# Expert rows turned by transposing transfers instead of TensorE, and another order of the last two batches' routing, in an attention and mixture-of-experts kernel

## The chip, the cores and the metric

The kernel runs on one core of a Trainium2 chip. The metric is the device time of one execution in microseconds (us). Engines are named as in the profile: PE (TensorE), PEld (its weight loads), DVE (VectorE), ACT (ScalarE), POOL (GpSimd) and SP (SyncE, which here only issues transfers).

## The reference

Chunked attention with memory keys, and then a mixture of experts with two experts for each token:

```
for each chunk c of 32 positions:              # 4 batches, 8 heads, 768 positions, head size 64
    keys   = 8 memory keys + positions c-16 .. c+32+8
    out[c] = softmax(q[c] @ keys.T / 8) @ values
x = out as 3072 rows of 512
noisy  = x @ w_gate + log1p(exp(x @ w_noise)) * noise          # 8 experts
top2   = the two largest of each row; gates = softmax over the two
y[row] = sum over its two experts e of gate * (relu(x[row] @ w1[e]) @ w2[e])   # w1 512x1024, w2 1024x512
```

## The kernel before, in words

**Attention** works in 16 pairs of heads (NPAIR = 16, four for each of the 4 batches), in a software pipeline written out by hand: the loop over `i` issues, for each engine in turn, steps of pairs `i+2`, `i+1`, `i`, `i-1` and `i-2`. For the change these matter, all of a pair `n`: `PT_pe` (L323) transposes the probabilities P on PE, `PT_dve` (L330) copies them out of PSUM, `PV_pe` (L335) multiplies them with the values, `mult_dve` (L349) divides by the sums and writes the rows `xrow`, `xT_pe` (L363) transposes these rows on PE and lets ACT copy them to `xt`, for the logits. The PSUM pool for transposes has three buffers, that for PV's result one.

**Routing** of a batch `b` starts with `logits_pe` (L374) and runs as small steps (`s1` to `s8`, L392 to L517): noise scale (`ns`, on ACT), noisy logits `nl`, comparison of all pairs of experts (`df`, `bt`), the two best (`two`), a one-hot `oh` over the 28 pairs of experts, ranks by matmuls with a triangular matrix (`s3`, `s5`), a table of places (`s5b` builds `Rn`, `s6` multiplies, `s7` adds to the running table `tab`), and the gates (`s4`), which are written to HBM with the rows. `s8` adds the batch's counts to `seen`. The steps of batches 0 to 2 hang in a list `pending` and are dealt out between the steps of the attention (`early_steps`, `late_steps`); those of the last batch run in one go after the last pair (L649 to L661).

**Buckets.** A token's two experts are one of 28 pairs, and each pair is a bucket of up to 128 rows. A bucket is fetched once: `gather` (L693, POOL) fetches its rows from HBM by index, `turn` (L701) transposes the 128 rows of 512 on PE in four pieces, DVE copies them to `xTb`, and ACT copies the gates to `meta`. The first 122 places of a bucket are its own; overflow goes to spill places that are handled apart.

**Experts** run in order 0 to 7. Each has seven buckets, in a big half (4) and a small half (3). `first` (L758) multiplies w1 with a half's rows (8 blocks of 128 hidden units, 4 matmuls each, into four PSUM buffers `ps_h`), and ACT and DVE take turns at the relu. `second` (L777) multiplies one bucket with w2; a bucket that comes for the first time is copied to one of 20 accumulators by ACT, one that comes for the second time is added by DVE and scattered to the output by POOL, with a small transfer `spart` by SP. Expert `e` meets 7, 6, 5, 4, 3, 2, 1 and 0 buckets that no expert before had (`plan[e]`). In the kernel before, expert `e` gathers `plan[e+1]` after its first products (L902 to L904), then loads w1 of expert `e+2`, turns one new bucket after each second product (L911), and loads w2 of expert `e+2` at its end. All gathers, scatters and weight loads are issued by POOL, in this order.

Of the kernel before, what the change touches and what calls it, by code (L numbers as in the profile page):

```python
# [24 lines left out]
def kernel(  # L25
# [73 lines left out]
    def body():  # L99
# [49 lines left out]
        def zero_v(x, j, eng=None):  # L149
            (eng or nc.vector).memset(vbufs[x][:, 6 * j:6 * j + 6], 0.0)  # L150
# [178 lines left out]

        def PT_dve(n):  # L330
            PT = ap_.tile([128, 2 * UB, 128], BF16, name="PT")
            nc.vector.tensor_copy(PT, st[n]["p_p"])  # L332
            st[n]["PT"] = PT

        def PV_pe(n):  # L335
# [27 lines left out]
        def xT_pe(n):  # L363
            b, r = divmod(n, HP)
            y, half = divmod(r, 2)
            p_x = psT.tile([128, UB, 2, 128], BF16, name="p_x", tag="tr")
            for u in range(UB):
                for s in range(2):
                    nc.tensor.transpose(out=p_x[:, u, s, :], in_=xrows[b][:, UB * half + u, 128 * y + 64 * s:128 * y + 64 * s + 64].bitcast(BF16), identity=identb)  # L369
            xt = ap_.tile([128, UB, 2, 128], BF16, name="xt", bufs=5)  # L370
            nc.scalar.copy(xt, p_x)  # L371
            st[n]["xt"] = xt

        def logits_pe(b):  # L374
# [12 lines left out]
        def route(b):  # L387
# [4 lines left out]
            def s1():  # L392
                ns = T("ns", [128, BT, E])
                ps_l = logits[b]
                nc.scalar.activation(out=ns, in_=ps_l[:, :, E:], func=Act.Exp)
                nc.scalar.activation(out=ns, in_=ns, func=Act.Ln, bias=1.0)
                R["ns"] = ns
                R["lg"] = T("lg", [128, BT, E])
                nc.scalar.copy(R["lg"], ps_l[:, :, :E])

# [34 lines left out]
            def s2b():  # L435
                over = T("over", [128, BT, E])
                nc.vector.tensor_reduce(out=over, in_=R["bt"], axis=AX, op=Alu.add)
                two = T("two", [128, BT, 2, E], BF16)
                nc.vector.tensor_scalar(out=two, in0=over.rearrange("p t (o e) -> p t o e", o=1).to_broadcast([128, BT, 2, E]),
                                        scalar1=2.0, scalar2=None, op0=Alu.is_lt)  # L440
                oh = T("oh", [128, BT, E // 2, E], BF16)
                tw = two.rearrange("p t o e -> p t (o e)")
                pitch = tw.ap[1][0]
                win = bass.AP(tw.tensor, tw.offset + 1, [list(tw.ap[0]), [pitch, BT], [1, E // 2], [1, E]])
                side.tensor_tensor(out=oh, in0=two[:, :, 0:1, :].to_broadcast([128, BT, E // 2, E]), in1=win, op=Alu.mult)
                R["two"] = two[:, :, 0, :]
                R["oh"] = oh.rearrange("p t d e -> p t (d e)")

# [120 lines left out]
        def late_steps():  # L569
            if pending:  # L570
                for fn in pending.pop(0)[1]:
                    fn()
# [18 lines left out]
        for i in range(NPAIR):  # L591
            if i >= 1:
                PT_pe(i - 1)
            max_dve(i)
            for n in ahead(i):
                qkT_pe(n)
            fresh = i >= 3 and (i - 3) % HP == HP - 1
            if fresh:
                begin_route((i - 3) // HP)
            early_steps()  # L600
            if i >= 1:
                PT_dve(i - 1)
            sub_dve(i)
            if i == 0:
                zero_v(1, 1)
                load_v(1)
                new_group(3)
                load_qk(3)
            if i == 1:
                zero_k(3)  # L610
            for n in ahead(i):
                kT_act(n)
            if i >= 1:
                PV_pe(i - 1)
            if i + 1 < NPAIR:
                scores_pe(i + 1)
            if i < NPAIR - 1:
                late_steps()
            if i in (2, 3, 4):
                zero_v(2, i - 2)  # L620
            if i >= 1:
                mult_dve(i - 1)
                if i - 1 == NPAIR - 2:
                    write_rows(B, B - 1, 0, UB, 0, XC)
            if i >= 2:
                xT_pe(i - 2)
            if i == 2:
                load_v(2)
                memory_values(2, NG)
            for n in ahead(i):  # L630
                g = n // GP + 3
                if n % GP == 1 and g < NG:
                    new_group(g)
                    load_qk(g)
            if i == 3:
                zero_v(2, 3, nc.gpsimd)
                ramps()
                load_router()
            if i == 4:
                load_v(3)  # L640
            if i == 5:
                constants()
            if i >= 4 and i % GP == 0 and i // GP + 2 < NG:
                load_v(i // GP + 2)
            if i == GP * (NG - 3) + 1:
                load_w1(0)
                load_w2(0)
                load_w1(1)
        n = NPAIR - 1  # L649
        PT_pe(n)  # L650
        PT_dve(n)
        xT_pe(n - 1)
        late_steps()
        PV_pe(n)
        mult_dve(n)
        write_rows(B + 1, B - 1, UB, BT, 0, XC)
        early_steps()
        xT_pe(n)
        late_steps()
        begin_route(B - 1)  # L660
        late_steps()  # L661


        tab = tabs[(B - 1) % 2]
        gidx = rp.tile([128, NB], I32, name="gidx")
# [35 lines left out]
        def turn(p, other=False):  # L701
            xl = got[p]
            p_t = psY.tile([128, KP, CAP], BF16, name="p_t2", tag="ps_y") if other else psX.tile([128, KP, CAP], BF16, name="p_t")
            for kp in range(KP):
                nc.tensor.transpose(out=p_t[:, kp, :], in_=xl[:, kp * 64:(kp + 1) * 64].bitcast(BF16), identity=identb)  # L705
            nc.vector.tensor_copy(xTv[:, :, p, :], p_t)  # L706
            nc.scalar.copy(meta[:, p, :], xl[:, XC:].bitcast(F32))

        def gather_spill(s_gi):
            xl = ld.tile([128, ROW], I32, name="xl")  # L710
# [166 lines left out]
        for e in range(E):  # L877
            big, small = halves(e)
            if e == E - 1:
                end = nc.values_load(n_spill_i[0:1, 0:1], min_val=SPILL, max_val=N)  # L880
                past = xg.tile([128, NP], F32, name="past")
                nc.vector.tensor_scalar(out=past, in0=srank, scalar1=-float(SPILL), scalar2=None, op0=Alu.add)
            ht = hp_.tile([128, FB, (E - 1) * CAP], BF16, name="ht")
            if e == 0:
                parts = [big[:2], big[2:], small]
                off = 0
                for x, ps in enumerate(parts):
                    for j, p in enumerate(ps):
                        turn(p, j % 2 == 1)
                    if x == 2:  # L890
                        turn_spill()
                        find_tails()
                    first(W1[e], ht, off, ps, nc.scalar if x == 0 else None, CAP if x == 2 else OWN, big if x == 2 else ())
                    off += len(ps)
                    if x == 0:
                        s_gi, s_si = find_spill()
                        gather_spill(s_gi)
                        load_w2(1)
            else:
                first(W1[e], ht, 0, big)  # L900
                first(W1[e], ht, len(big), small)
            nxt = list(plan[e + 1]) if e + 1 < E else []  # L902
            for p in nxt:
                gather(p)  # L904
            if e + 2 < E:
                load_w1(e + 2)
            order = big + small

            for j, p in enumerate(order):
                second(e, p, ht, j, W2[e])  # L910
                if nxt:  # L911
                    turn(nxt.pop(0))
                if e == E - 1 and j == 1:
                    for x in range(1, E // 2 - 1):
                        nc.vector.tensor_tensor(out=spart[:, 0, :], in0=spart[:, 0, :], in1=spart[:, x, :], op=Alu.add)
            if e == E - 1:
                assert color(order[-1]) >= NCOL
                nc.vector.tensor_tensor(out=spart[:, 0, :], in0=spart[:, 0, :], in1=spart[:, E // 2 - 1, :], op=Alu.add)
                nc.gpsimd.indirect_dma_start(
                    out=out_part[NB], out_offset=bass.IndirectOffsetOnAxis(ap=s_si[:, 0:1], axis=0),  # L920
                    in_=spart[:, 0, :], in_offset=None, bounds_check=N - 1, oob_is_err=False)
            while nxt:
                turn(nxt.pop(0))
            if e + 2 < E:
                load_w2(e + 2)
        return end, past, ovc, ramp_i, onesb, identb, psX, psY, first, ld, hp_, xg, accs, load_w1, load_w2, W1, W2, relu, psH
# [87 lines left out]
```

## Time and profile before

| | |
|---|---|
| median of 3 runs | 337.96 us (335.78 to 338.23) |
| profiled execution | 335.33 us |
| its span in the profile | 333.7 us |
| granted TensorE clock, mean | 0.957 |
| attention and routing, up to the first gather | 0 to 114.2 us |
| expert 0 starts its first products | 119.8 us |
| experts 1, 2, 3 start | 152.6, 177.9, 203.1 us |
| bytes moved by DMA | 42.99 MB, mean 129 GB/s |

How to read it: the span is the time from the first to the last instruction in the trace of one execution. A group of instructions is named by its line, engine, operation and tiles (written<-read). "Idle before" is the time that the engine stood still just before, and the arrow names what ended that. The chain of waits follows the work back from the last instruction, always to what released it; "issue" in it is time in which nothing in the profile was waited for. In windows of the trace, times are us from the span's start.

### The profile page before, as it was taken

The page shows a single profiled execution, that of the slowest core. Times are in us where ns is not written, and L with a number is a line of the kernel's source. Part 1 is how long each engine was busy: PE and PEld are TensorE (multiplying, and loading weights), DVE is VectorE, ACT ScalarE, POOL GpSimd, SP SyncE. Part 2 cuts the span into 40 slices and gives each one's busy share as a digit, 9 for nine tenths or more (in the row PEclk, how much of TensorE's full clock was granted, in tenths as well). Part 3 has the DMA queues.
Part 4 walks back from the last instruction along what each step waited for, and adds up shares of the span by engine and source line. Part 5 has one row for each costly group of instructions (what it writes and reads, how often), then busy time and mean ns, then how long its engine had stood idle before and what let it go on. Part 6 is the DMA issues. An engine that isn't in the chain of part 4 may idle for free.

```text
span 333.7 us, 7301 instructions
## 1 busy us (share of the span) xinstructions
PE 288.1 (86%) x3019; PEld 173.5 (52%) x3019; DVE 169.9 (51%) x343; ACT 133.4 (40%) x235; POOL 138.6 (42%) x181
## 2 busy tenths in 40 slices
PE   1697887977776377999999999999999999999990
PEld 0575675755654256554754754544544544544540
DVE  7789859849958775222322323424342433434451
ACT  7877788757433033533333332332303303202200
POOL 7877868538023472781008007007152042042152
PEclk9999999979989559999999999999999999999997
DMA  7999999999997136699407905914959624521031
GB/s 99 179 163 176 184 163 163 210 143 101 214 225 216 23 88 93 128 156 238 87 0 125 221 4 110 223 28 105 207 147 166 117 111 70 86 109 60 1 140 71
DMA packets 58763, 42.99 MB, mean 129 GB/s; under 512 B 32449, under 2 KB 52033, under 8 KB 58728
## 3 DMA queue, kind: packets, MB, share of 16 engines
q0 software_dynamic: 49808, 38.71, 77.0%
q1 hardware_dynamic: 8632, 3.74, 5.6%
q8 instruction: 24, 0.39, 0.5%
q10 hardware_dynamic: 288, 0.07, 0.1%
q14 instruction: 11, 0.09, 0.1%
HBM read 61.23 MB, written 10.66 MB: 215 GB/s over the span
## 4 chain that ended last, share of the span: by engine, by line
PE 43%; issue 24%; DVE 13%; ACT 8%; POOL 7%; DMA 3%; POOLq 0%; DVEq 0%; ACTq 0%
PE ps_h L769 16%; PE ps_y L780 14%; POOL out_dram L788 4%; ACT kd L276 3%; PE ps_o L345 3%; DMA out_dram<-acc,sidx 2%; PE ps_o L341 2%; DVE mx L313 2%; DVE xrow L358 2%; DVE sd L318 2%; DVE vg L150 2%; PE p_t L705 2%; ACT xt L371 1%; ACT P L320 1%; PE p_t L265 1%
## 5 line engine op out<-in xcount | busy, mean ns | idle before, releaser
L769 PE MATMUL ps_h<-xTb,w1t 128*128 128x512 bf16 (+5 forms) x640 | 101.4, 320 | 1.5 <-DVE xTb L706 1.5
L780 PE MATMUL ps_y<-w2t,ht 128*128 128x512 bf16 x448 | 101.4, 379 | 0.0
L769 PEld LDWEIGHTS <-w1t 128*128 128x128 bf16 x640 | 58.6, 99 | 43.9 <-DVE xTb L706 1.1
L788 POOL DMA_INDIRECT out_dram<-acc,sidx x28 | 28.1, 1004 | 126.4 <-DVE acc L787 124.1
L756 DVE TENSOR_SCALAR ht<-ps_h 128x512 bf16<-128x512 f32 (+3 forms) x68 | 38.1, 560 | 68.1 <-PE ps_h L769 63.1
L780 PEld LDWEIGHTS <-ht 128*128 128x128 bf16 x448 | 42.9, 98 | 46.7
L754 ACT ACTIVATE ht<-ps_h 128x384 bf16<-128x384 f32 (+2 forms) x76 | 38.9, 511 | 70.4 <-PE ps_h L769 66.3
L784 ACT ACTIVATE acc<-ps_y,meta 128x512 f32<-128x512 f32 x28 | 19.2, 687 | 62.6 <-PE ps_y L780 45.4
L787 DVE SCALAR_TENSOR_TENSOR acc<-ps_y,meta,acc 128x512 f32<-128x512 f32 x28 | 21.0, 750 | 34.5 <-PE ps_y L780 34.5
L696 POOL DMA_INDIRECT xl<-x_rows,gidx x28 | 30.0, 1071 | 16.8 <-PE ps_h L769 6.6
L134 POOL DMA_DIRECT2D vg<-in_v_dram x34 | 25.5, 756 | 11.4 <-DMA kg<-in_k_dram 3.7
L706 DVE COPY xTb<-p_t 128x512 bf16<-128x512 bf16 x28 | 11.6, 422 | 28.6 <-PE p_t L705 28.4
L276 ACT COPY kd<-p_t 64x768 bf16<-64x768 bf16 x32 | 25.2, 786 | 1.0 <-PE p_t L265 0.8
L265 PE MATMUL p_t<-identb,qg 128*64 128x128 bf16 x192 | 10.3, 245 | 12.0 <-DMA qg<-in_q_dram 6.6
L371 ACT COPY xt<-p_x 128x768 bf16<-128x768 bf16 x16 | 12.8, 798 | 12.0 <-PE p_x L369 11.9
L341 PE MATMUL ps_o<-memv,PT 128*128 128x260 bf16 x96 | 15.0, 296 | 2.2 <-DVE PT L332 2.0
L320 ACT ACTIVATE P<-sd 128x768 bf16<-128x768 f32 x16 | 13.5, 845 | 8.1 <-DVE sd L318 8.1
L268 ACT COPY qT<-p_t 128x768 bf16<-128x768 bf16 x16 | 12.8, 800 | 8.9 <-PE p_t L265 8.8
L358 DVE TENSOR_TENSOR xrow<-ps_o,rec 128x768 bf16<-128x768 f32 x16 | 15.3, 958 | 0.6
L313 DVE TENSOR_REDUCE mx<-ps_s 128x12 f32<-128x768 f32 x16 | 15.1, 942 | 0.5 <-PE ps_s L300 0.5
L318 DVE TENSOR_TENSOR sd<-ps_s,mx 128x768 f32<-128x768 f32 x16 | 15.2, 949 | 0.0
L345 PE MATMUL ps_o<-vg,PT 128*32 128x256 bf16 x384 | 14.9, 293 | 0.0
(150 smaller groups left out, 287.5 us busy)
## 6 DMA issues: line engine op xcount, KB each, us to landing
w1t<-in_moe_w_dram POOLq DMA_DIRECT2D x8, 1024.0 KB, 11.4
w2t<-in_moe_w_dram POOLq DMA_DIRECT2D x8, 1024.0 KB, 10.1
vg<-in_v_dram POOLq DMA_DIRECT2D x30, 168.0 KB, 10.2
qg<-in_q_dram POOLq DMA_DIRECT2D x7, 384.0 KB, 9.9
kg<-in_k_dram POOLq DMA_DIRECT2D x7, 384.0 KB, 11.3
x_rows<-xrow SPq DMA_DIRECT2D x3, 792.0 KB
x_rows<-xrow SPq DMA_DIRECT2D x2, 384.0 KB
xl<-x_rows,gidx POOLq DMA_INDIRECT x28, 6.5
```

Of the source, the lines that this page charges most:

```text
L134: nc.gpsimd.dma_start(out=vg[p0 + j:p0 + j + nj, c:c + n, hd, :, :].rearrange("p c e d -> p c (e d)"), in_=bass.AP(v.tensor, v.offset + (g ...
L276: nc.scalar.copy(st[n]["kT"][hs, hh, :].rearrange("d (p j) -> d p j", j=SJ), st[n]["p_k"][hs].rearrange("d j p -> d p j"))
L313: nc.vector.tensor_reduce(out=mx, in_=st[n]["ps"], axis=AX, op=Alu.max)
L318: nc.vector.tensor_tensor(out=sd, in0=st[n]["ps"], in1=bc4(st[n]["mx"], CTX), op=Alu.subtract)
L345: nc.tensor.matmul(out=po[32 * r:32 * r + 32, u, :MD], lhsT=PT[:, 2 * u + e, 32 * r:32 * r + 32], rhs=vg[:, CB * half + x, :, e, :], start ...
L358: nc.vector.tensor_tensor(out=xr.rearrange("p u (h d) -> p u h d", d=D), in0=po[:, :, :MD].rearrange("p u (h d) -> p u h d", d=D), in1=rec ...
L696: nc.gpsimd.indirect_dma_start(out=xl, out_offset=None, in_=xd, in_offset=bass.IndirectOffsetOnAxis(ap=idx[:, p:p + 1], axis=0), bounds_ch ...
L754: nc.scalar.activation(out=dst, in_=src, func=Act.Relu)
L756: nc.vector.tensor_scalar(out=dst, in0=src, scalar1=0.0, scalar2=None, op0=Alu.max)
L769: nc.tensor.matmul(out=ps_h[:, o:o + w], lhsT=w1t[:, kp, f * 128:(f + 1) * 128], rhs=rhs(kp), start=(kp == 0 and i == 0), stop=(kp == KP - ...
L780: nc.tensor.matmul(out=ps_y, lhsT=ht[:, f, j * CAP:(j + 1) * CAP], rhs=w2t[:, f, :], start=(f == 0), stop=(f == FB - 1))
L788: nc.gpsimd.indirect_dma_start(out=out_part[p], out_offset=bass.IndirectOffsetOnAxis(ap=sidx[:, p:p + 1], axis=0), in_=a, in_offset=None, ...
```

## The change

Two edits that have nothing to do with each other.

1. Buckets of experts 2 to 6 are no longer turned on PE. `turn_far` gathers a bucket and lets SP issue four transposing transfers from the gathered rows straight into `xTb`; it is called two experts ahead, where `turn` was called one expert ahead (`plan[1]` stays with `turn`). In expert 0 the first two such buckets come before the second products. ACT copies the gates of these buckets at the expert's end. w1 of expert `e+2` is now loaded ahead of the gathers.
2. In the seam between attention and experts, the order of batch 2's and batch 3's routing is written out: batch 2's `s1m`, `s2a`, `s2g` ahead of `mult_dve` of pair 14, the others between the last pair's steps, `s6` after the last logits and `s7` inside batch 3's steps. The transpose of rows of pair 13 goes behind P's of pair 15. P of pair 15 is copied by ACT, one third of the last `xt` by DVE. The last batch's logits are read from PSUM without a copy, and its one-hot is made by POOL instead of DVE.

```
         def PT_dve(n):
-            nc.vector.tensor_copy(PT, st[n]["p_p"])
+            (nc.scalar.copy if n == NPAIR - 1 else nc.vector.tensor_copy)(PT, st[n]["p_p"])
...
         def xT_pe(n):
-            nc.scalar.copy(xt, p_x)
+            own = UB - 1 if n == NPAIR - 1 else UB
+            nc.scalar.copy(xt[:, :own], p_x[:, :own])
+            if own < UB:
+                nc.vector.tensor_copy(xt[:, own:], p_x[:, own:])
...
             def s1():
+                if b == B - 1:
+                    R["lg"] = ps_l[:, :, :E]
+                    return
...
             def s2b():
-                side.tensor_tensor(out=oh, ...)
+                nc.gpsimd.tensor_tensor(out=oh, ...)
...
+            if i == NPAIR - 1:
+                s1m, s2a, s2g, s2b, s4b, s3, s4, s5, s5b, s6, s7, s8 = [f for pair in pending for part in pair for f in part]
+                pending.clear()
+                s1m()
+                s2a()
+                s2g()
             if i >= 1:
                 mult_dve(i - 1)
...
-            if i >= 2:
+            if 2 <= i < NPAIR - 1:
                 xT_pe(i - 2)
...
         PT_pe(n)
         PT_dve(n)
-        xT_pe(n - 1)
-        late_steps()
+        xT_pe(n - 2)
+        s2b()
+        s4b()
+        s4()
         PV_pe(n)
         mult_dve(n)
         write_rows(B + 1, B - 1, UB, BT, 0, XC)
-        early_steps()
+        xT_pe(n - 1)
+        s3()
+        s8()
+        s5()
         xT_pe(n)
-        late_steps()
-        begin_route(B - 1)
-        late_steps()
+        s5b()
+        logits_pe(B - 1)
+        begin, (_, (s1n, s1m, s2d, s2a, s2g, s2b, s4b, s3, s4, s5, s5b, *last)) = route(B - 1)
+        begin()
+        s6()
+        for f in (s1n, s1m, s2d, s2g, s2a, s2b, s4b, s7, s3, s4, s5, s5b, *last):
+            f()
...
+        def turn_far(p):
+            gather(p)
+            for kp in range(KP):
+                nc.sync.dma_start_transpose(out=xTv[:, kp, p, :], in_=got[p][:, kp * 64:(kp + 1) * 64].bitcast(BF16))
...
-            nxt = list(plan[e + 1]) if e + 1 < E else []
+            nxt = list(plan[1]) if e == 0 else []
             for p in nxt:
                 gather(p)
+            far = list(plan[e + 2]) if e + 2 < E else []
             if e + 2 < E:
                 load_w1(e + 2)
+            if e == 0:
+                for p in far[:2]:
+                    turn_far(p)
...
             for j, p in enumerate(order):
                 second(e, p, ht, j, W2[e])
                 if nxt:
                     turn(nxt.pop(0))
+                late = j + 2 if e == 0 else j
+                if late < len(far):
+                    turn_far(far[late])
...
-            while nxt:
-                turn(nxt.pop(0))
+            for p in far:
+                nc.scalar.copy(meta[:, p, :], got[p][:, XC:].bitcast(F32))
             if e + 2 < E:
                 load_w2(e + 2)
```

More of the change, by code (lines that the diff above doesn't have):

```diff
@@ L444, in s2b @@
                 win = bass.AP(tw.tensor, tw.offset + 1, [list(tw.ap[0]), [pitch, BT], [1, E // 2], [1, E]])
-                side.tensor_tensor(out=oh, in0=two[:, :, 0:1, :].to_broadcast([128, BT, E // 2, E]), in1=win, op=Alu.mult)
+                nc.gpsimd.tensor_tensor(out=oh, in0=two[:, :, 0:1, :].to_broadcast([128, BT, E // 2, E]), in1=win, op=Alu.mult)
                 R["two"] = two[:, :, 0, :]
```

## The prediction

> **What bounds the kernel now.** I read the page first (engine shares, the 40 slices), then the busy time by stage, then the chain of waits inside the expert stage, then the timeline of the seam between attention and experts, and last the transfers by window. The page, parts 1 and 2:
>
> ```profile
> PE 288.1 (86%) x3019; PEld 173.5 (52%) x3019; DVE 169.9 (51%) x343; ACT 133.4 (40%) x235; POOL 138.6 (42%) x181
> ...
> PE   1697887977776377999999999999999999999990
> ...
> PEclk9999999979989559999999999999999999999997
> DMA  7999999999997136699407905914959624521031
> ```
>
> A slice is 8.34 us. From slice 16 on (133 us) PE is full; slices 12 to 15 (100 to 133 us) are the seam. By stage (busy us and instructions of PE, PEld, DVE, ACT, POOL, then clock, DMA share, GB/s):
>
> ```profile
> 107.00:114.24 7.24, 2.02 (x26) 1.58 (x27) 6.32 (x28) 0.24 (x1) 1.15 (x2) 0.51 0.25 70
> ...
> 152.40:177.90 25.50, 25.50 (x174) 14.73 (x173) 7.78 (x14) 8.91 (x19) 2.19 (x3) 1.00 0.45 101
> 177.90:203.10 25.20, 25.20 (x170) 14.43 (x168) 8.21 (x14) 8.13 (x17) 6.45 (x7) 1.00 0.61 116
> ```
>
> Two regimes. In the seam (first row) DVE works 6.32 of 7.24 us in a serial chain and PE idles. In the experts PE is busy for all 25.5 and 25.2 us of experts 1 and 2: there, only PE time taken away counts, or a new wait of PE. The chain of waits there:
>
> ```profile
> 152.55 12.19 PE ps_h L769 x96
> 164.74 1.73 PE ps_y L780 x8
> 166.47 0.22 PE p_t L705 x4
> 166.69 1.73 PE ps_y L780 x8
> ...
> 174.49 3.45 PE ps_y L780 x16
> 177.94 12.19 PE ps_h L769 x96
> ...
> 197.93 5.18 PE ps_y L780 x24
> 203.11 3.02 PE ps_h L769 x14
> ```
>
> An expert is 12.19 us of first products and seven second products of 1.73 us; each block of rows turned on PE (four p_t transposes) adds 0.22 us, with no gap.
>
> **The change, part 1: blocks of experts 2 to 6.** New blocks per expert are 7, 6, 5, 4, 3, 2, 1, 0; so 5+4+3+2+1 = 15 turns leave PE. Each is 0.22 us on the chain: 15 x 0.22 = 3.3 us gained. The 15 copies of xTb leave DVE, which waits for PE there and gives nothing. ACT's copies of the gates (meta) stay, moved to an expert's end. The ends of the kernel (last scatters) follow PE and move with it.
>
> What it adds: 15 x 4 = 60 transposing transfers on SP's queue, of which this trace has none. Call T the time from one to the next. What T must be follows from the start and the deadlines, so I look at loads and gathers. Timeline of POOL, then DMA issues of five windows (141 to 143.5 us, 143.5 to 150.3, 182.5 to 184, 134 to 142, last column landing time), then SP's timeline, the size of its meta transfers, its L548, and last the end of expert 3 in the whole chain:
>
> ```profile
> 141.94 0.83 POOL L538 DMA_DIRECT2D w1t<-in_moe_w_dram  x1
> ...
> 149.42 1.01 POOL L696 DMA_INDIRECT xl<-x_rows,gidx  x1 [0.30 <-issue]
> ```
> ```profile
> w2t<-in_moe_w_dram POOLq DMA_DIRECT2D x1, 1024.0 KB, 13.1
> ```
> ```profile
> xl<-x_rows,gidx POOLq DMA_INDIRECT x5, 10.2
> ```
> ```profile
> w1t<-in_moe_w_dram POOLq DMA_DIRECT2D x1, 1024.0 KB, 10.0
> ```
> ```profile
> xl<-x_rows,gidx POOLq DMA_INDIRECT x6, 2.9
> ```
> ```profile
> 128.79 4.70 SPq L730 DMA_DIRECT2D meta<-xl  x6
> ```
> ```profile
> meta<-xl SPq DMA_DIRECT2D x6, 0.2 KB
> ```
> ```profile
> L548 SPq DMA_DIRECT2D x_rows<-xrow x6: 359/362/371, 58.8 to 111.2; - x6
> ```
> ```profile
> 221.07 6.91 PE ps_y L780 x32
> ```
>
> Start. In the kernel before, expert 2's gathers go out at 144 to 150 us behind both weight loads and land 10.2 us later. Now only w1 of expert 2 lies ahead (issued 141.94, landing some 10.0 later, 152); w2 goes behind the gathers. With the seam's 0.8 us (part 2) the first gather lands near 151 to 152, the last near 155.5 (estimate: five of them in the 4 us or so that they took behind w2, which landed at 142.74 + 13.1 = 155.9). So transposing starts at about 152, and from there the queue always has work: expert 1's first four steps scatter nothing, so POOL runs on into expert 3's gathers.
>
> Deadlines. Expert 2's big half needs four blocks, 16 transfers, at 177.94 - 0.8 - 5 x 0.22 = 176.0: T up to (176.0 - 152)/16 = 1.50 us. Its fifth block is due 7 us later: 31/20 = 1.55. Expert 3 has all four new blocks in its big half, 36 transfers in all, due at 203.11 - 0.8 - 9 x 0.22 = 200.3: T up to 48.3/36 = **1.34 us**, the tightest. Expert 4's three are in its small half, 48 transfers by about 221.07 + 6.91 - 0.8 - 12 x 0.22 + 5 = 229: 1.6. So up to T = 1.34 all is hidden; beyond it PE stalls 36 us for each us of T, and at T = 1.34 + 3.5/36 = 1.44 the gain is gone.
>
> Bounds of T from rows: below, SP's own 0.36 us per issue of a big transfer (L548); above, 2.9 us, a gather that lands with nothing ahead of it, as if each transfer waited for the one before. Nearest by queue, size and issue back to back are the six meta transfers, 4.70/6 = 0.78 us. I take T below 1.34, near that row and not near 2.9, and cost it at nothing on PE; the cover is expert 1 and half of expert 2, and with it gone the price is that of rival 2. A transposing transfer of 32 KB has more to do than a 0.2 KB one, so both ends stay in the range.
>
> The Trainium skill ("VectorE: DVE Perf Modes", section "The three transpose paths") gives 390 ns for a 128x128 bf16 transpose on TensorE and 1309 ns through DMA. The trace disagrees on the first: four of them cost 0.22 us on the chain, so 60 would be worth 23.4 us by the page and 3.3 by the row, and the row decides. On the second no row speaks; with it 152 + 36 x 1.309 = 199.1 would be 1.2 us ahead of expert 3, an estimate that leaves the sum as it is.
>
> SP's queue carries also the 24 spart transfers; those of expert 1 stand behind expert 3's transposes. Their readers are the reuse of an accumulator two experts on and the sum in expert 7, so nobody is late.
>
> A wait that is added: ACT's gate copies at the end of expert 0 stand ahead of expert 1's relus and wait for the last gather, near 155.5. PE starts expert 1 at 152.55 - 0.8 and fills four ps_h in 4 x 12.19/16 = 3.0 to 3.5 us, by 155.2; the first relu (ACT's) then ends near 156.3. The stall is 0 to 1.1 us: I take 0.6. For later experts the gathers go out ten and more us before the copies: nothing.
>
> **Part 2: the seam.** Rows of the timeline:
>
> ```profile
> 97.31 0.84 ACT L320 ACTIVATE P<-sd 128x768 bf16<-128x768 f32 x1 [2.22 <-DVE sd L318]
> ...
> 98.91 0.82 PE L369 MATMUL p_x<-identb,xrow 128*128 128x128 bf16 x6
> ...
> 99.52 0.85 PE L327 MATMUL p_p<-identb,P 128*128 128x128 bf16 x6
> ```
> ```profile
> 99.77 0.80 ACT L371 COPY xt<-p_x 128x768 bf16<-128x768 bf16 x1 [1.61 <-PE p_x L369]
> ...
> 100.41 0.56 DVE L332 COPY PT<-p_p 128x768 bf16<-128x768 bf16 x1
> ...
> 102.69 0.51 POOL L445 TENSOR_TENSOR oh<-two 128x192 bf16<-128x192 bf16 x1 [7.63 <-DVE two L439]
> ...
> 102.98 0.96 DVE L358 TENSOR_TENSOR xrow<-ps_o,rec 128x768 bf16<-128x768 f32 x1
> ...
> 104.54 0.80 ACT L371 COPY xt<-p_x 128x768 bf16<-128x768 bf16 x1 [2.72 <-PE p_x L369]
> ...
> 105.53 1.07 DVE L480 TENSOR_SCALAR Rn<-ramp,rank_all 128x128 bf16<-128x128 bf16 x6
> ...
> 106.14 0.24 ACT L396 ACTIVATE ns<-ns 128x48 f32<-128x48 f32 x1
> ...
> 106.90 0.19 DVE L503 TENSOR_TENSOR tab<-ps_t,tab 128x28 f32<-128x28 f32 x1 [0.31 <-PE ps_t L495]
> 107.01 0.20 DVE L407 TENSOR_TENSOR nl<-ns,nz_all 128x48 f32<-128x48 f32 x1
> ...
> 109.93 0.27 DVE L445 TENSOR_TENSOR oh<-two 128x192 bf16<-128x192 bf16 x1
> ...
> 114.24 1.19 POOL L696 DMA_INDIRECT xl<-x_rows,gidx  x1 [2.82 <-DVE ov L807]
> ```
>
> - P copy by ACT, p_x of pair 13 behind it: P is ready at 98.15, so p_p starts near 98.95 instead of 99.52. ACT copies in 0.80 (as its xt row) where DVE took 0.56 but came only at 100.41: PT at 100.6 instead of 100.97, 0.35 us gained, carried on to the last xrow (103.94 to 103.6).
> - Batch 2's s1m and s2a go into DVE's idle time before 99; s2b and s4 fill the time up to the last xrow: nothing.
> - The last xt is shared, 512 columns on ACT (0.6 by the 0.80 row's share) and 256 on DVE: 0.2 us, so logits come 0.55 us early. The logits are no longer copied; ns, which ended at 106.38, ends near 105.85.
> - s7 leaves its place before the last batch's nl, which waited for Rn (to 106.60), s6 and tab (106.90). Now nl follows ns and Rn: 105.9 instead of 107.01, 1.1 us gained. s7 lies under the one-hot, where DVE idles.
> - The one-hot by POOL: 0.51 instead of 0.27, on the path to rank: 0.3 us lost with the hand-over. oht and ohp follow later on POOL, still before Rn ends.
>
> Sum: 1.1 - 0.3 = 0.8 us gained at the first gather (114.24); bounds 1.6 (nothing lost on POOL, the 0.5 of s6 and tab wholly off) and -0.3 (s5 and Rn of batch 2, now ahead of nl on DVE, hold it).
>
> **Sum.** 3.3 + 0.8 - 0.6 = 3.5 us. The profiled execution took 335.33 us (span 333.7): 331.8. It stands 2.6 us under the median of 337.96; the same step from the median gives **334.4**.
>
> **Rivals.**
> 1. Half eaten: T between 1.34 and 1.5, or the full ACT wait and no gain in the seam. A stall of 36 x 0.1 = 3.6 us takes the whole gain: 335 to 341. For it: the slack at expert 3 is nothing, and slices 18 and 19 show the DMA engines busy at 9 and 9 tenths in the start. Against: over the whole of expert 1 their share is 0.45.
> 2. Slower, by one mechanism: expert 3's first products wait for transposes that are still queued on SP. Decides from T = 1.44. At T = 1.8: expert 2 waits 152 + 28.8 - 176.0 = 4.8, its small half 0.2, expert 3 then 152 + 64.8 - 205.3 = 11.5; net of the 3.5 it is 351. At T = 2.9, each waiting for the one before, 22.4 + 4.6 + 29.1 + 5.6 = 61.7, so 396. For 2.9: the lone gather. Against: SP's six meta transfers follow each other in 0.78 us, so plain ones don't wait for each other. The Trainium skill speaks for this rival ("DMA: Bandwidth & Descriptors", section "Rules for kernel authors"): under 64 KB a transfer pays mostly overhead, and these are 32 KB. The six meta rows agree, 0.78 us for 0.2 KB.
> 3. The transposes hide and the seam gives more (1.6) with no ACT wait: 337.96 - 4.9 = 333.1.
>
> **How the numbers follow.** About 1% is what a measurement of this kernel can tell from no change. Forecast with rival 3 (331.5 to 336): 0.47; rival 1: 0.17; rival 2 up to T = 1.8: 0.18; beyond: 0.18. The range leaves out only the last: 331.5 to 351. The forecast's own range is 331.5 to 336; as 1% faster lies at 334.6, a part of it is "same". Faster by over 1%: 0.42; within 1%: 0.20; slower: 0.38.
>
> **What would show it.** Chain of waits: ps_y to ps_y at 1.73 with no p_t after expert 0, and no DMA or SP wait ahead of ps_h of experts 2 and 3; if rival 2 holds, PE has gaps just there, largest at expert 3, and the last transpose of a block lands as the gap ends. SP's rows give T by the distance of starts. ACT's meta copy in expert 0 shows a DMA wait, and a PE gap of up to 1.1 us near 155. In the seam nl starts at 105.9 and the first gather at 113.4. Wrong if T is over 1.44 us, or if the transposes slow the weight loads, which have ten us to spare.

## The result, and the profile after

The changed kernel takes 334.52 us (median of 9 runs, 331.49 to 335.92), the kernel before 337.58 (9 runs, 335.78 to 340.04): a ratio of 0.9896, 95% interval 0.9865 to 0.9927, so 1.0% faster (0.7 to 1.4%). The prediction was 334.4.

The two profiled executions can't be compared as wholes. That of after took 335.92 us, the slowest of its kernel's nine runs; that of before took 335.33, less than any of the nine runs of its kernel beside it (335.78 at the least). So I read them stage by stage. First the page of after, parts 1 and 2, for the lines shown of before:

```profile
PE 287.7 (86%) x2959; PEld 171.6 (51%) x2959; DVE 163.4 (49%) x327; ACT 133.3 (40%) x235; POOL 139.0 (42%) x182
...
PE   1687987988875488699999999999999999999990
...
PEclk9998999899978569979999999999999999999998
DMA  7999999999997228489934974964969724521032
```

The 60 transposes are gone from PE (3019 to 2959 instructions). A new dent stands in PE at slice 16 and in its clock at slice 17 (counted from 0; 134 to 150 us). It lies in expert 0, where PE's work is the same in both kernels; it has its own experiment below. Experts 1 and 2 in the table by stage, then the second products of expert 1 in the chain of waits, both of after:

```profile
156.04:180.31 24.27, 24.27 (x153) 13.51 (x152) 5.75 (x9) 8.85 (x19) 3.52 (x5) 1.00 0.70 125
180.31:204.59 24.28, 24.28 (x154) 13.55 (x152) 6.50 (x10) 8.06 (x17) 5.33 (x6) 1.00 0.82 137
```
```profile
159.87 8.52 PE ps_h L794 x79
168.39 12.10 PE ps_y L805 x56
```

The 25.50 and 25.20 us of experts 1 and 2 are now 24.27 and 24.28, with PE as full as before. The 56 second products run in one piece of 12.10 us, seven times 1.73, with no p_t between. Now the new transfers, in SP's timeline and in the answer for their line (duration in ns: least, median, most; start of the first and of the last):

```profile
149.17 49.96 SPq L732 DMA_TRANSPOSE xTb<-xl  x36
```
```profile
L732 SPq DMA_TRANSPOSE xTb<-xl x60: 1116/1230/3016, 149.2 to 252.3; - x60
```

A row of SP is the issue of a transfer: it doesn't hold the time until the data have landed. SP issues the first 36 one behind the other in 49.96 us, 1.39 us each: most follow the one before in 1.28 us, and a few take up to 3.0 us. The seam, rows of the timeline of after, and one row of before that the prediction did not show:

```profile
98.03 0.96 DVE L358 TENSOR_TENSOR xrow<-ps_o,rec 128x768 bf16<-128x768 f32 x1
98.48 0.80 ACT L332 COPY PT<-p_p 128x768 bf16<-128x768 bf16 x1 [1.65 <-PE p_p L327]
...
104.65 0.20 DVE L413 TENSOR_TENSOR nl<-ns,nz_all 128x48 f32<-128x48 f32 x1
...
111.95 1.18 POOL L716 DMA_INDIRECT xl<-x_rows,gidx  x1 [2.57 <-DVE void L688]
```
```profile
99.31 0.96 DVE L358 TENSOR_TENSOR xrow<-ps_o,rec 128x768 bf16<-128x768 f32 x1
```

The first row of each is xrow of pair 14, where the new order begins. It starts anywhere from 96.6 to 99.5 us in the traces of this study, whatever the kernel, so I count from it. Before, nl came 107.01 - 99.31 = 7.70 us later and the first gather 14.93; after, 6.62 and 13.92.

All traces of the study by stage, in us. Expert 0 is the time from its first product to that of expert 1; the last column reaches from there to the end of the span. Labels are explained with the experiments.

| kernel | xrow of pair 14 to first gather | expert 0 | expert 1 to the end |
|---|---|---|---|
| before | 14.93 | 32.58 | 181.35 |
| e6 (before) | 14.74 | 37.12 | 181.34 |
| e1, e11 (seam alone) | 13.85, 13.85 | 32.21, 37.27 | 181.32, 181.34 |
| e2 (transfers alone) | 14.73 | 32.18 | 180.93 |
| e12 (transfers alone, w1 behind) | 14.70 | 38.77 | 178.02 |
| after | 13.92 | 38.55 | 178.07 |
| e3, e9 (after) | 13.85, 13.84 | 32.93, 36.08 | 178.04, 178.07 |
| e5, e10 (after, w1 behind) | 13.85, 13.85 | 38.68, 38.94 | 178.01, 178.01 |

The last column gives the 3.3 us of the turns to a tenth, with one exception (e2). The first gives 0.9 us for the seam (1.0 between before and after, the two traces that lie furthest from the others). The middle one moves by up to 7 us, in the kernel before (32.58, 37.12) as in the changed one.

### The profile page after: what moved, and what is told of

Read it like the earlier page. It is cut to its first block, busy times and chain, and to the rows that moved or that the text cites. A ratio compares the mean times of both kernels' runs of the same rounds, so it can differ in the third digit from the quotient of the medians.

```text
span 334.1 us, 7270 instructions
## 1 busy us (share of the span) xinstructions
PE 287.7 (86%) x2959; PEld 171.6 (51%) x2959; DVE 163.4 (49%) x327; ACT 133.3 (40%) x235; POOL 139.0 (42%) x182
## 4 chain that ended last, share of the span: by engine, by line
issue 38%; PE 25%; DVE 15%; POOL 8%; ACT 8%; DMA 4%; another core or an unknown queue 1%; POOLq 1%; DVEq 0%; ACTq 0%
PE ps_h L794 9%; PE ps_y L805 7%; POOL out_dram L813 5%; ACT kd L276 3%; DMA out_dram<-acc,sidx 2%; DVE mx L313 2%; PE ps_o L345 2%; DVE xrow L358 2%; DVE vg L150 2%; DVE sd L318 2%; PE ps_o L341 2%; POOL xl L716 2%; ACT P L320 1%; ACT xt L372 1%; PE p_t L265 1%
## 5 line engine op out<-in xcount | busy, mean ns | idle before, releaser
L805 PEld LDWEIGHTS <-ht 128*128 128x128 bf16 x448 | 43.7, 98 | 55.4 <-DVE ht L781 4.5
L779 ACT ACTIVATE ht<-ps_h 128x384 bf16<-128x384 f32 (+2 forms) x76 | 38.9, 511 | 74.1 <-PE ps_h L794 67.3
L372 ACT COPY xt<-p_x 128x768 bf16<-128x768 bf16 (+1 forms) x16 | 12.6, 785 | 9.7 <-PE p_x L369 9.4
L265 PEld LDWEIGHTS <-qg 128*64 128x64 bf16 x192 | 7.8, 126 | 12.1 <-DMA qg<-in_q_dram 6.8
```

Of the source, the lines that this page charges most:

```text
L265: nc.tensor.transpose(out=p_t[64 * hh:64 * hh + 64, j, :], in_=src[:, 2 * i + hh, j * D:(j + 1) * D], identity=identb)
L779: nc.scalar.activation(out=dst, in_=src, func=Act.Relu)
L805: nc.tensor.matmul(out=ps_y, lhsT=ht[:, f, j * CAP:(j + 1) * CAP], rhs=w2t[:, f, :], start=(f == 0), stop=(f == FB - 1))
```

## The experiments

The theory: the time falls by PE's 15 turns (3.3 us) and by the seam (0.8), and the transfers are ready before their readers, since one follows the other in less than 1.34 us, the limit that the prediction works out. The rival: transfers are ready too late in part, and PE gives back at experts 2 and 3 what it gained.

### Each part alone, and the whole again

e1 is the second edit alone (all of the new routing order, with `turn` and `plan[e + 1]` as before); e2 is the first edit alone; e3 is the changed kernel again. They ran on one chip, where the kernel before takes 332.82 us.

```
e1:  lines of the new order from the changed kernel, experts from the kernel before
e2:  + def turn_far(p): ...        + far = list(plan[e + 2]) ...        routing from the kernel before
```

> The kernel before with the new order of the last two batches' routing alone; all blocks of rows are turned on PE. Theory (the parts add up, each on its own stretch): the first gather comes 0.8 to 1.0 us earlier after pair 14's PV than before, the expert stage is as before, so about 1 us less than before (336.6 where before takes 337.6). Rival (the seam's gain is lost again while expert 0 waits for gathers and spill places, which POOL and DVE do in series): no difference. Rival (the stop of ACT in expert 0, 138.6 to 140.9 us in the changed kernel's trace, comes from the new order): the stop shows here too, and the time is 3 to 5 us above before.

> The kernel before with the transposing transfers alone; the seam is the old one. Theory (parts add): experts 1 to 5 are shorter by 1.1, 0.9, 0.7, 0.4 and 0.2 us, 3.3 us in all, so about 334.3 where before takes 337.6. Rival (36 transfers at 1.38 us from 149.2 are done at 199 to 200 us, just when expert 3 starts; where expert 0 has no stop they are late): a gap of PE of 1 to 4 us ahead of expert 3, and only 0 to 2 us gained. Rival (the stop in expert 0 comes from the transfers or from w1's load going ahead of the gathers): it shows here, with PE idle some 3 us near 139 to 143 us, and the gain is gone.

> The changed kernel as it is, for a second profile of it. If the stop of ACT in expert 0 (2.4 us, then PE at half its clock for some 3 us: 5.8 us in all against before) belongs to the kernel, it shows again and the time is 334 to 336. If it comes in some executions only, as the spread from 331.5 to 335.9 over nine runs would have it, it is missing here, expert 1 starts near 150.5, and expert 3 would start near 199: then the 36 transposing transfers, done near 200, leave a PE gap of up to 2 us there, by the deadline that the prediction worked out, or none if they start earlier too.

Measured: e1 332.59 us, ratio 1.0004 (0.9971 to 1.0037). e2 331.43, 0.9950 (0.9913 to 0.9987). e3 330.37, 0.9956 (0.9921 to 0.9991). The mechanism shows best in e3's chain of waits, experts 1 and 2, and in a row of its SP:

```profile
150.84 12.19 PE ps_h L794 x96
...
163.30 10.74 PE ps_y L805 x49
...
175.12 12.19 PE ps_h L794 x96
...
187.57 10.74 PE ps_y L805 x49
...
199.39 4.75 PE ps_h L794 x22
```
```profile
149.46 48.07 SPq L732 DMA_TRANSPOSE xTb<-xl  x36
```

There is nothing but products in the chain: neither a transpose nor a wait for a transfer. In e2's profiled execution it went otherwise. Its PE timeline around experts 2 and 3, and two pieces of its chain:

```profile
174.79 7.51 PE L774 MATMUL ps_h<-xTb,w1t 128*128 128x512 bf16 x37
182.65 0.33 PE L774 MATMUL ps_h<-xTb,w1t 128*128 128x128 bf16 x2 [0.35 <-DMA xTb<-xl]
184.23 4.83 PE L774 MATMUL ps_h<-xTb,w1t 128*128 128x128 bf16 x57 [1.26 <-DMA xTb<-xl]
...
200.99 0.81 PE L774 MATMUL ps_h<-xTb,w1t 128*128 128x512 bf16 x3
201.96 1.25 PE L774 MATMUL ps_h<-xTb,w1t 128*128 128x512 bf16 x5 [0.17 <-DMA xTb<-xl]
```
```profile
197.98 1.23 SPq L712
...
199.25 2.67 DMA xTb<-xl
```

Expert 4 starts 226.15 - 174.79 = 51.36 us after expert 2, in e3 223.42 - 174.95 = 48.47: 2.9 us of the 3.3 are given back. This execution took 333.40 us, 2.0 above the median of e2's twelve, so what it lost isn't what e2 loses as a rule. The queue is 1.9 us later than in e3 (first transfer at 151.34, there 149.46), and it is late twice. Expert 3's last transfer, the 36th, is issued at 199.25 and lands 2.67 us later, at 201.92; expert 3 was due at 174.79 + 24.27 = 199.06. And the fifth bucket of expert 2, whose four transfers SP issued from 173.49 to 177.56, isn't late by its issue at all. By the semaphore records of the trace its transfers land at 178.47, 181.61, 182.60 and 184.19, 5.0 to 6.9 us after their issue; PE's waits end at 182.65 and 184.23. POOL's timeline and the table by stage of e2 show what they met:

```profile
173.66 0.99 POOL L543 DMA_DIRECT2D w2t<-in_moe_w_dram  x1
174.61 0.83 POOL L538 DMA_DIRECT2D w1t<-in_moe_w_dram  x1
```
```profile
174.79:178.00 3.21, 3.21 (x16) 1.47 (x15) 0.69 (x1) 1.98 (x7) 2.60 (x3) 1.00 0.77 96
178.00:184.00 6.00, 4.62 (x25) 2.22 (x24) 2.08 (x3) 1.37 (x3) 1.22 (x2) 1.00 1.22 200
184.00:190.00 6.00, 5.72 (x62) 4.87 (x63) 2.23 (x4) 1.96 (x4) 0.00 (x0) 1.00 1.13 204
```

Two weight loads of 1 MB and three gathers go out between 173.66 and 179.5, and from 178 to 190 the DMA engines are full (share 1.22 and 1.13, 200 and 204 GB/s). The transfers of that stretch take up to 9.4 us to land, those just ahead of it and behind it 2.2 to 2.7. The first ten, issued from 151.34 to 163 us with the DMA engines as full (share 1.18 from 151 to 158), took 5.8 to 10.9. The loads are the cause as far as the times coincide, stretch by stretch; no run took them away. They are slowed as well, but by less: from the issue of w2 at the end of an expert to the landing of the next w1 it takes 16.3 us (expert 1) and 15.9 (expert 2) in before, with gathers between the two, 16.7 and 18.0 in e2, 16.4 and 17.0 in e3. In e3 the same happens with the queue 1.9 us ahead: the 20th transfer lands at 182.10, where expert 2 takes up its small half, and the 36th at 198.66, 0.56 us ahead of expert 3. So both the theory and the rival are seen: in these two executions the transfers are ready just in time and just too late.

e1's trace shows the seam's gain, its time does not:

```profile
98.08 0.96 DVE L358 TENSOR_TENSOR xrow<-ps_o,rec 128x768 bf16<-128x768 f32 x1
...
111.93 1.19 POOL L716 DMA_INDIRECT xl<-x_rows,gidx  x1 [2.58 <-DVE void L688]
```

From 98.08 to 111.93 are 13.85 us, 0.9 less than the 14.70 to 14.93 of the four traces with the old order. What was gained isn't taken back up to expert 1, which starts 37.74 us after the first gather in e1 and 37.75 in e2. A gain of 0.9 would be a ratio of 0.9973, still within e1's interval.

### How near is the edge: every transfer twice, and one expert ahead

e4 issues each transposing transfer twice, first into a tile that nobody reads. e8 makes them one expert ahead instead of two, so that a bucket has about 24 us less.

```
e4:  for kp in range(KP):
+        nc.sync.dma_start_transpose(out=spare[:, turned[0] % 16, :], in_=got[p][...])
         nc.sync.dma_start_transpose(out=xTv[:, kp, p, :], in_=got[p][...])
e8:
-    far = list(plan[e + 2]) if e + 2 < E else []
+    far = list(plan[e + 1]) if 0 < e < E - 1 else []
-    if e == 0:
-        for p in far[:2]:
-            turn_far(p)
```

> The changed kernel with every transposing transfer issued twice, the first time into a spare tile that nobody reads: 120 transfers, so 2.76 us for each that is needed. Theory (SP's queue works them off one after the other at 1.38 us, and the experts wait for theirs): from a start at 149.2, 16 needed ones are done at 193.4 where expert 2 starts at 180.5 (gap 13 us), 20 at 204.4 (4 us more), 36 at 248.6 (27 us ahead of expert 3), 48 at 281.7 (4 us in expert 4); in all 48 us, about 382. Rival (1.38 us is what SP takes to issue, and the engines' work is hidden in some other way, so that the queue doubles its rate): 334.5 to 345. Rival (each transfer's landing is what spaces them): the same as the theory, but the spacing in the trace differs between a transfer into the spare tile and one into the rows.

> The changed kernel with the transfers one expert ahead, as the turns on PE were, instead of two. Theory (1.28 us each, and the start decides): expert 2's gathers land near 160 behind w2 and w1, its first 16 transfers are done at 181 where PE is there at 175, a gap of about 6 us; expert 3's gathers go out only behind expert 1's scatter, land near 191, the 16 are done at 212 where PE is there at 205, a gap of about 7; later experts nothing. So some 13 us above the changed kernel, 343. Rival (an expert of 24 us is enough for 20 transfers at 1.28, so one expert ahead does as well): within 2 us of the changed kernel.

Measured: e4 394.36 us, 1.1849 (1.1755 to 1.1944); e8 364.33, 1.0806 (1.0745 to 1.0867). Both signs are as expected, both sizes too small. PE's waits in e4, rows of its timeline, and its table by stage:

```profile
PE ps_h L799 <- DMA xTb<-xl: 42.6, 6, 19.4
PE ps_y L810 <- ACT acc L814: 11.4, 1, 11.4
```
```profile
189.14 1.44 PE L799 MATMUL ps_h<-xTb,w1t 128*128 128x512 bf16 x3 [16.28 <-DMA xTb<-xl]
...
238.44 1.25 PE L799 MATMUL ps_h<-xTb,w1t 128*128 128x512 bf16 x2 [19.37 <-DMA xTb<-xl]
...
278.40 4.85 PE L810 MATMUL ps_y<-w2t,ht 128*128 128x512 bf16 x11 [11.45 <-ACT acc L814]
```
```profile
189.00:193.00 4.00, 2.82 (x7) 0.98 (x8) 0.00 (x0) 0.60 (x1) 0.51 (x1) 0.50 0.26 61
238.40:246.00 7.60, 3.56 (x8) 1.02 (x9) 0.00 (x0) 0.60 (x1) 0.00 (x0) 0.50 0.12 23
```

The gaps stand where rival 2 of the prediction puts them, ahead of experts 2 and 3. From one expert's start to the next, expert 1 lasts 40.71, expert 2 49.30 and expert 3 45.88 us in place of 24.27, 24.28 and 24.19: 63.1 us lost. The waits above are 54.0 of them; most of the rest is the lower clock told of below. I had left out two things. The wait of 11.45 us is one step removed: ACT, about to overwrite an accumulator, stood 13.39 us until `spart<-acc` had landed, and that small transfer was queued behind the transposes on SP. And after each long gap PE runs at half its clock (0.50 in both windows). The Trainium skill ("TensorE: Matmul & The Clock Gate", Part 1) has half rate as the state that PE falls into when idle; the rows agree.

e8, the same two views of PE and a row of its table:

```profile
PE ps_h L794 <- DMA xTb<-xl: 19.1, 10, 5.2
```
```profile
186.10 14.46 PE L794 MATMUL ps_h<-xTb,w1t 128*128 128x512 bf16 x93 [4.51 <-DMA xTb<-xl]
...
220.60 0.61 PE L794 MATMUL ps_h<-xTb,w1t 128*128 128x512 bf16 x1 [5.18 <-DMA xTb<-xl]
```
```profile
186.00:190.00 4.00, 3.90 (x10) 1.39 (x10) 0.69 (x1) 0.60 (x1) 0.00 (x0) 0.50 1.29 180
```

Experts 2, 3 and 5 last 35.21, 33.79 and 33.11 us in place of 24.28, 24.19 and 24.19, together 29.4 us lost: 19.1 of waiting, the rest mostly the half clock behind the gaps (estimate: 8 us, half of the 16 us or so that PE worked at clock 0.50 there). The waits at experts 2 and 3, 6.5 and 7.0 us, are as large as forecast; the four of expert 5, 5.6 us together, and the clock were not in the forecast. The 16th transfer was issued at 179.17 and landed at 186.05, with the DMA engines full again (share 1.03 from 180 to 186); the wait ends at 186.10. I had counted issues and not landings, the same omission as in e2. Two experts ahead isn't caution: one expert ahead, with the gathers behind w1 and dealt out between the second products as here, costs 8%. One expert ahead with all gathers ahead of w1, as in the kernel before, wasn't tried.

### Expert 0, and an earlier start of the transfers

If the transfers are just in time, an earlier start should help. e5 and e10 (one kernel, on two chips) load w1 of expert 2 behind the five gathers of expert 0, not ahead of them; e12 does so with the old seam. e6 is the kernel before, e9 the changed kernel, e11 the seam alone again.

```
-            if e + 2 < E:
+            if 0 < e < E - 2:
                 load_w1(e + 2)
...
                     turn_far(far[late])
+                if e == 0 and late == len(far) - 1:
+                    load_w1(2)
```

> The changed kernel, but w1 of expert 2 is loaded behind all five gathers of expert 2's blocks instead of ahead of them. In the three traces with the transfers, the first gather landed only at 149.2 to 151.3 us, behind 1 MB of w1, and where it was 151.3 (the transfers alone) PE stood some 3 us ahead of experts 2 and 3; where it was 149.5 the 36th transfer was issued at 196.3 and expert 3 had nothing to spare. Theory (the start of the queue decides, by 1.28 us each behind it): here the first transfer starts near 145 to 146 us, the 36th is done near 193, 6 us before expert 3; no execution has a gap, and the median is 0.5 to 1.5 us below the changed kernel (ratio to before about 0.992 where that had 0.9956). Rival (w1 of expert 2, now some 6 us later, becomes late): a gap ahead of expert 2 for w1t, and no gain. Rival (lateness is rare): the same time as the changed kernel.

> The kernel before as it is, for a second profile of it beside those of the experiments. Theory: from the last but one xrow (pair 14) to the first gather it takes 14.7 to 14.9 us, against 13.85 to 13.95 with the new order; experts 1 to 4 take 25.4, 25.2, 24.9, 24.6 us again. What differs before the seam (pair 14's xrow came at 99.3 in the kernel before and at 96.8 to 98.4 in the others) is no effect of the change and moves by a us or two from one execution to the next.

> The changed kernel once more, beside the two that follow. Theory (the trace's terms are 0.9 us from the seam and 3.3 from the experts, 4.2 in all; where PE does not stop in expert 0 some executions lose 1 to 3 us of it again because the transposing transfers come too late for expert 2 or 3, and where it does stop, expert 0's stage is 0.7 to 2.3 us longer than before's): ratio to before 0.990 to 0.996. The profile tells which of the two it is: expert 1 starts 19.4 us after the last products of expert 0 begin (no stop) or 24 to 27.

> The changed kernel with w1 of expert 2 behind the gathers, once more. Theory (late transfers cost something only where expert 0 has no stop): where it has none, the transfers begin near 143 and the time is 1 to 2 us below the changed kernel's, ratio to before about 0.988; where it stops, the same as the changed kernel's within 0.5 us. Rival (the transfers are never late in a typical execution): the same in both cases.

> The new order of the routing alone, once more, to narrow its worth: the first time gave a ratio of 1.0004 with an interval of 0.33% to each side, while its trace shows 0.9 us less from pair 14's xrow to the first gather (13.85 against 14.73 to 14.93). Theory (the trace's 0.9 us is in the time): 0.9973. Rival (the gain is taken back between the first gather and expert 1): 1.000, and the stretch from the first gather to expert 1's start is 0.9 us longer than before's 37.75 to 38.15 us.

> The old order of the routing with the transposing transfers, w1 of expert 2 behind the gathers. Theory (3.3 us from the experts, all of it, with nothing late): ratio 0.990, and no gap ahead of experts 2 and 3, where the same with w1 ahead had gaps of 1.5 and 1.3 us. Rival (the gaps come from something else than the late start): they show here too.

Measured, e5 and e6 on one chip, the other four on another: e5 335.61 us, 0.9942 (0.9908 to 0.9976); e6 337.69 in its one run; e9 333.78, 0.9889 (0.9838 to 0.9941); e10 334.86, 0.9914 (0.9871 to 0.9957); e11 336.95, 0.9995 (0.9958 to 1.0032); e12 337.25, 0.9983 (0.9947 to 1.0019). e9 lies just beside its forecast of 0.990 to 0.996, well within the interval. The earlier start is there, in SP's timeline of e5:

```profile
142.29 52.28 SPq L732 DMA_TRANSPOSE xTb<-xl  x36
```

That is 6.9 us ahead of after, and PE waits for no transposing transfer in e5, e10 or e12. Nothing is won all the same: e10 isn't faster than the changed kernel beside it (0.9914, e9 0.9889), and e5, whose chip ran no changed kernel, misses its forecast of 0.992. e12 has no gap ahead of experts 2 and 3 and gains the 3.3 us in the table of stages (178.02), but not in its time: 0.9983 where 0.990 was forecast. The reason that shows lies in expert 0, 38.7, 38.9 and 38.8 us in the table of stages, where e6, the kernel before, has 37.1. What makes it so long isn't the change alone, as ACT's rows of the relu in expert 0 show, of before, of e6 (the same kernel on another chip), and of after, the last with the row of PE that makes the products:

```profile
138.40 0.49 ACT L754 ACTIVATE ht<-ps_h 128x384 bf16<-128x384 f32 x1 [0.26 <-PE ps_h L769]
```
```profile
139.63 0.49 ACT L754 ACTIVATE ht<-ps_h 128x384 bf16<-128x384 f32 x1 [2.40 <-remote]
```
```profile
130.96 6.17 PE L794 MATMUL ps_h<-xTb,w1t 128*128 128x384 bf16 x64
```
```profile
135.88 0.49 ACT L779 ACTIVATE ht<-ps_h 128x384 bf16<-128x384 f32 x1 [1.03 <-PE ps_h L794]
138.06 0.49 ACT L779 ACTIVATE ht<-ps_h 128x384 bf16<-128x384 f32 x1 [1.69 <-PE ps_h L794]
140.91 0.49 ACT L779 ACTIVATE ht<-ps_h 128x384 bf16<-128x384 f32 x1 [2.36 <-remote]
```

In the first trace each relu follows PE's products at once; the idle time of 0.26 us is the wait for the next ones. In the other two ACT stands still for 2.4 us, and the profile has no releaser for it ("remote"; in after's chain the same piece is called another core or an unknown queue, 2.34 us). By PE's rows the products were there: its last ones end at 137.13. The stop isn't one wait, either. Of ACT's last eight relus in expert 0 the first three are on time and the next five fall behind in steps, in after by 0.2, 1.0, 2.4, 4.5 and 4.5 us against PE's rows; the view puts some of these waits down to PE, as the first two rows of after show. PE runs dry, and the clock falls, here in the table by stage of e6 and of after:

```profile
142.00:144.00 2.00, 2.00 (x6) 0.76 (x5) 0.38 (x1) 0.40 (x2) 1.60 (x2) 0.50 1.02 176
```
```profile
140.00:146.00 6.00, 3.96 (x14) 1.56 (x15) 0.79 (x3) 1.75 (x4) 3.88 (x4) 0.75 0.87 140
```

Without this stop expert 0 lasts 32.2 to 32.9 us, with it 36.1 to 39.4, in the kernel before as in the changed one. It is absent from the first trace of before, and from those of e1 to e4 on the chip where the kernel before takes 332.82 us. It is present in the trace of after, and in all eight of the chips where the kernel before takes 337.91 and 337.53, e6 and e11 with the turns on PE among them. The last relu is then 3.7 to 4.5 us late, and 5.1 to 5.2 in the four traces with w1 behind (e5, e7, e10, e12). So w1 behind seems to lengthen it; whether the change makes it more frequent, two traces of the kernel before and three of the changed one can't tell. ACT's view of waits has 2.7 us of it in e6, 2.6 in e9 and, here, 4.0 in e5 (two stops, the longer 2.4):

```profile
ACT ht L779 <- remote: 4.0, 2, 2.4
```

So where the stop occurs, PE comes to expert 2 late by itself and the transfers have time. After's 36th transfer landed at 200.25, 4.3 us ahead of expert 3; an earlier start can't win there. w1 behind wasn't tried on a chip without the stop, and what ACT waits for isn't settled.

### The one-hot on DVE

e7 is e5 with the last batch's one-hot back on DVE.

```
-                nc.gpsimd.tensor_tensor(out=oh, ...)
+                side.tensor_tensor(out=oh, ...)
```

> As the kernel with w1 behind the gathers, and the last batch's one-hot on DVE again (0.27 us there, 0.51 on POOL). Theory (POOL's one-hot costs the path 0.3 us): from pair 14's xrow to the first gather 13.6 us instead of 13.9; the time is 0.3 us lower at most, which the medians can hardly tell. Rival (DVE's tab and the gates, which lay under POOL's one-hot, now stand in the path): 13.9 or more.

Measured: 335.92 us, 0.9934 (0.9902 to 0.9967), not to be told from e5. Its seam in the timeline:

```profile
97.91 0.96 DVE L358 TENSOR_TENSOR xrow<-ps_o,rec 128x768 bf16<-128x768 f32 x1
...
107.39 0.27 DVE L451 TENSOR_TENSOR oh<-two 128x192 bf16<-128x192 bf16 x1
...
111.70 1.18 POOL L716 DMA_INDIRECT xl<-x_rows,gidx  x1 [2.81 <-DVE ov L832]
```

From xrow to the gather are 13.79 us, with POOL's one-hot 13.85: POOL costs 0.06 us there.

## Why the prediction was right, point by point

- **15 turns at 0.22 us.** Right: expert 1 to the end is 181.3 us in every trace with the turns on PE, and 178.0 to 178.1 in every one without them but e2, e4 and e8, where transfers are late.
- **T below 1.34 us.** Right for one transfer and the next, 1.28 us from issue to issue (rows of 1.23), not for the 36 together: a few longer ones make it 48.1 to 50.0 us, 1.34 to 1.39 each. The choice near the 0.78 us of the small transfers was too low. The figure of a page, 1309 ns (the Trainium skill, "VectorE: DVE Perf Modes", section "The three transpose paths"), comes near the 1.28 us of the rows. The 36 then have to land, 2.2 to 2.7 us at best, a term that the prediction left out. From its 152 us all this would have been late. That it came out well is luck: the queue started at 149.2 and 149.5 us in after and e3, some 2.7 us ahead of the forecast, and that paid for the landing; after had the late PE of expert 0 besides. In e2 the queue started at 151.3, near the forecast, and was late.
- **The deadlines** were worked out for issues. The landing beside weight loads, 5 to 9 us there, is missing, and it makes the fifth bucket of expert 2 as tight as expert 3. The prediction asked whether the transposes slow the loads. They do, by 0.1 to 2.1 us; the transposes beside the loads lose more, up to 8.6 us each, which it did not ask. (The two slices in which it saw the DMA engines at 9 tenths are 17 and 18 by its own count, not 18 and 19.)
- **Half eaten** (rival 1) took place in e2's profiled execution, nearly whole: 2.9 us of 3.3.
- **Rival 2** has its mechanism right (e4: gaps ahead of experts 2 and 3), and its condition isn't met. Its price left out the clock and the accumulators that wait for `spart`.
- **ACT's gate copies, 0.6 us.** Not there: in e3 they start at 151.53 without a wait, and the next relu at 152.01; in e2 they wait for a gather for 0.3 us and PE notices nothing.
- **The seam, 0.8 us.** 0.9 by the traces. nl gains 7.70 - 6.62 = 1.1 between before and after, as predicted, but 0.9 between all other traces (7.46 to 7.49 us with the old order, 6.54 to 6.56 with the new); POOL's one-hot takes back less than 0.1, not 0.3. No timing shows it for sure. The seam alone has 1.0004 and 0.9995, together 1.0000 give or take 0.0025 (estimate from the two intervals), so that 0.9973 is just outside. Beside the transfers it is worth nothing in e3 against e2 (0.9956, 0.9950) and 2.4 us in e10 against e12.
- **The sum** by the traces is 3.3 + 0.9 = 4.2 us, the forecast had 3.5, and measured were 337.58 - 334.52 = 3.1; as ratios 1.0%, 0.4% (e3) and 1.1% (e9). So the mechanism of the 3.3 us is shown, and that 334.4 meets 334.52 to 0.1 us is luck. The smallest gain is on the chip without the stop, where e2 was late and e3 had 0.56 us in hand; that other executions there are late like e2's fits, but each kernel has one profile on that chip, so it isn't shown. Where the missing 1 us of the other chips goes stays open; expert 0 differs by more than that between traces of one kernel (38.55 in after, 36.08 in e9).

## What to carry to other kernels

Work taken from a full engine is worth its time on the chain, here 0.22 us for four transposes, and that held to a tenth here; what can spoil it is whether the substitute is ready. For a queue of transfers count the landing, not the issue, and count it beside whatever else the DMA engines carry in that stretch: here 2.3 us became 9.4 to 10.9 beside weight loads. And when a gain is 1%, read it from stages that both traces have undisturbed: one stop in a stage whose work the change leaves alone (3 to 7 us here) can be larger than the whole change.

## What the runs showed of the hardware

- Transposing transfers of 32 KB are issued from one queue every 1.28 us as a rule, to either of two tiles alike (e4: median row 1.23 us for both). They land 2.2 to 2.7 us after the start of their issue when little else runs, and 5 to 10.9 us after it when the DMA engines are full (e2).
- After gaps of PE of 4.5 us and more, its granted clock was 0.50 for 4 us and longer (e4, e8). Four gaps of 1.3 to 1.5 us, one soon after the other, did the same (e8, expert 5: 0.50 from 285 to 289 us), the two of 0.35 and 1.26 us in expert 2 of e2 did not (1.00). A gap that lowers the clock costs more than its length: e8 lost 29.4 us for 19.1 us of waits.
- ACT fell 3.7 to 5.2 us behind PE's products (by PE's rows) over the last five of eight relus at one place of expert 0, with no single stop longer than 2.4 us, in all eight executions that were profiled on two chips and in none of four on a third. No row names the cause.
